# Linear attention beside a squared-ReLU layer: shorter warm-up, another start-up order, and two bursts moved ahead of the first gate pair

## The chip, the cores and the metric

One NeuronCore of a Trainium2 chip runs the whole program. The metric is the device time of one execution in microseconds. The times given are a median over several runs; the profile is one more execution, with every instruction recorded.

## What is computed

The input has 2048 tokens of 448 features. After a layernorm, one branch is linear attention with 16 heads of 28 features, the other a dense layer of 1792 units with a squared ReLU, whose output passes a SiLU and gates the first branch. The sum with the input is returned.

```python
xn = layernorm(x)                                  # no scale, no shift
q, k, v = split(xn @ wqkv)                         # 16 heads of 28
phi = lambda t: where(t > 0, t + 1, exp(t)) + 1e-6
kv, z = einsum("bhsd,bhse->bhde", phi(k), v), sum_s(phi(k))
s = ((phi(q) @ kv) / (phi(q) @ z + 1e-6)) @ wo     # heads joined before wo
h = relu(xn @ w1 + b1) ** 2
g = silu(h @ w2 + b2)
return x + s * g
```

## The kernel before

The 2048 tokens are 16 tiles of 128, and four groups (g = 0 to 3) of four tiles. For each tile the kernel needs the normalised tokens transposed, `xT`: 448 features are three chunks of 128 and a rest of 64, which is stored twice so that it can sit in either half of the partitions. `w1` is cut by output into 14 units `H0` to `H13` of 128, the queries into `Q0` to `Q2`, the keys into one unit `K` per tile.

**How work is written down.** The class `Program` holds operations with the tiles that they read and write. `place()` puts them on the engines. The order on TensorE (PE) and on the DMA queue of SyncE (SP) is the order of the calls in the source. On VectorE (DVE), ScalarE (ACT) and GpSimd (POOL) a planner picks the next operation by estimated times: by the time at which the result is due (`late`), or by a priority (`prio`) where one is given; `lead` moves a due time earlier, `after` adds a dependency, and `mode` of a DMA is the rate that the planner reckons with. Some operations may go to either DVE or ACT. The eight PSUM banks are given out by the planner too. `emit()` then writes the instructions with semaphore waits. So a changed estimate moves instructions, and no others change.

**The stages around the change, in order of time:**

- *Warm-up.* `warm(n)` issues n matmuls of 512 columns on constants (L976), nine at once and two behind the statistics of tile 0.
- *Tiles 0 to 3.* x arrives tile by tile (`load_x`), the first 768 columns of w1 by rows (`load_rows`), all from SP but the first rows and b1, which ACT issues. For each tile DVE takes the statistics (L409, L412), ACT makes `rstd` (a logarithm, L417, and an exponential, L421), DVE normalises (L427), PE transposes three chunks (L470), and DVE and ACT copy them out of PSUM into `xT` (L478). `h_tile(si)` then multiplies tile si with chunks c = 0, 1, 2 of w1 for the six units H0 to H5 at once (L996), six matmuls of 128 columns for each c; the next tile's transposes are called between c = 1 and c = 2. `h_rests` adds the 64-row rests (L1011).
- *Tiles 4 to 15.* `ln_group(g)` does statistics and normalisation on DVE, two tiles at a time, and transposes by DMA from SP (L455), one DMA for two tiles. The DMAs that are called before it stand ahead of it in SP's queue.
- *Bursts.* `fours("Q0 Q1|Q2 H3'", 0)` runs four units in both halves of PE's rows, in four parts of 8, 8, 6 and 6 matmuls (L610 for H, L552 for K, L576 for Q; the prime means the next group). It takes four PSUM banks. An H unit is followed by a relu on ACT (L592; for H0 to H5 of group 0 it may be on DVE, L589) and a square (DVE L598 or ACT L599); a K or Q unit by an exponential on ACT (L530) and two operations on DVE (L535, L540).
- *Gates.* `gates(a, c, inside)` computes h @ w2 for two tiles in two parts of 28 matmuls (L863), with a burst called between the parts. The first pair needs all of group 0's squared units and all 14 row blocks of w2. `g_out` (L844) adds b2 on DVE.

The order after the heads was:

```python
load_w2(0, 7, [pr.writer["xT3"]])
ln_group(1, lambda: load_w2(7, 14))   # the second half of w2 between the two transposes
load_x(8, 12)
late_loads()
fours("H6 H7|H10 H11", 0)
...
fours("Q0 Q1|Q2 H3'", 0)
g01 = gates(0, 1, lambda: fours("K4 H0|K5 H4", 1))
fours("H1 Q0|H5 Q1", 1)
```

Of the kernel before, what the change touches and what calls it, by code (L numbers as in the profile page):

```python
# [9 lines left out]
P = 128  # L10
S, D, F = 2048, 448, 1792
# [25 lines left out]
class Program:  # L37
# [9 lines left out]
    def add(self, eng, emit, reads=(), writes=(), dur=0.2, alts=(), nbytes=0, mode=None, after=(), prio=None, lead=0.0):  # L47
        op = Op(eng, emit, reads, writes, {eng: dur, **dict(alts)}, mode, nbytes, after)
        for t in op.reads:
            w = self.writer.get(t)  # L50
            if w is not None:
                op.deps.add(w)
            self.readers.setdefault(t, []).append(op)
        for t in op.writes:
            w = self.writer.get(t)
            if w is not None and w is not op:
                op.deps.add(w)
            for r in self.readers.get(t, ()):
                if r is not op:
                    op.deps.add(r)  # L60
            self.writer[t] = op
            self.readers[t] = [r for r in self.readers.get(t, ()) if r is op]
        op.deps.discard(op)
        for d in op.deps:
            d.succ.append(op)
        op.prio, op.lead = prio, lead
        self.ops.append(op)
        return op
# [174 lines left out]
def bass_recurrent_scan__linear_attn_block__dense_activation_squared_relu__prompt_kernel(  # L243
    nc, A_x, A_wqkv, A_wo, B_x, B_w1, B_b1, B_w2, B_b2, out
):
    with ExitStack() as es:
        sb = lambda name, shape, dtype: es.enter_context(nc.sbuf_tensor(name, shape, dtype))
        bf, f32 = dt.bfloat16, dt.float32
        pr = Program()
        add = pr.add  # L250
# [16 lines left out]
        b2b = sb("b2b", [P, D], bf)  # L267
# [74 lines left out]
        def dma(eng, dst, src, writes, nbytes, reads=(), after=(), prio=None, rate=None):  # L342
            return add(
                eng, lambda e, _: e.dma_start(dst, src), reads, writes, 0.45 if eng == "sp" else 0.5, nbytes=nbytes,  # L344
                after=after, prio=prio, mode=rate,
            )

        def load_x(lo, hi):
            dma("sp", x_tok[:, lo:hi, :], x_r[:, lo:hi, :], [("x", i) for i in range(lo, hi)], (hi - lo) * P * D * 2)

        def load_main(w, src, name, lo, hi):
            dma(
# [4 lines left out]
        def load_rest(eng, w, src, name, half, lo, hi, prio=None):  # L357
            dma(eng, w[HALF[half], 3, lo:hi], src[384:448, lo:hi], [(name, half)], 128 * (hi - lo), prio=prio)

        add("act", lambda e, _: e.preload_act_table_set("natural_log_exp_and_others"), [], ["actw"], 0.05, prio=-9)  # L360
        def load_rows(eng, c, prio=None):
            dma(eng, w_1[:, c, 0:768], B_w1[c * P : (c + 1) * P, 0:768], [("w1a", "m", c)], 768 * 256, prio=prio)

        dma("act", b1r[:, :], B_b1.rearrange("(f p) -> f p", p=P), ["b1r"], F * 2, prio=-8.5)
        load_x(0, 1)
        load_rows("act", 0, -8)
        load_x(1, 2)
        load_rows("sp", 1)
        load_x(2, 3)
        load_rows("sp", 2)  # L370
        load_x(3, 4)
        load_rest("sp", w_1, B_w1, "w1a", 0, 0, 384)
        load_rest("sp", w_1, B_w1, "w1a", 1, 384, 768)
        load_x(4, 8)
        load_main(w_1, B_w1, "w1b", 768, 1792)
        load_rest("sp", w_1, B_w1, "w1b", 0, 768, 1280)
        load_rest("sp", w_1, B_w1, "w1b", 1, 1280, 1792)
# [3 lines left out]
        load_main(w_qkv, A_wqkv, "wq", 0, D)  # L381
        load_rest("sp", w_qkv, A_wqkv, "wq", 0, 0, D)
        load_rest("sp", w_qkv, A_wqkv, "wq", 1, 0, D)
        dma("sp", b2b[:, :], bass.AP(tensor=B_b2.tensor, offset=B_b2.offset, ap=[[0, P], [1, D]]), ["b2b"], P * D * 2)

        def load_w2(lo, hi, after=()):
            dma(
# [18 lines left out]

        def ln_stats(si, prio=None, after=()):
            add(
                "dve", lambda e, _: e.bn_stats(st6[:, si, :], x_tok[:, si, :]), [("x", si)], [("st", si)], 0.53,  # L409
                prio=prio, after=after,  # L410
            )
            add("dve", lambda e, _: e.bn_aggr(mv[:, si, :], st6[:, si, :]), [("st", si)], [("mv", si)], 0.07, prio=prio and 0.5)  # L412

        def ln_rstd(lo, hi, prio=None):
            c = slice(lo, hi)
# [9 lines left out]
        def ln_norm(si, prio=None):  # L425
            def norm(e, dst, src):
                return e.tensor_scalar(  # L427
                    out=dst, in0=src, scalar1=mv[:, si, 0:1], scalar2=rstd[:, si : si + 1], op0=ALU.subtract, op1=ALU.mult
                )

            add(
                "dve", lambda e, _: norm(e, xn[:, si, 0:D], x_tok[:, si, :]), [("x", si), ("mv", si), ("rstd", si)],
                [("xn", si)], 0.3, prio=prio,
            )
# [5 lines left out]
                [("xn", i) for i in ts], [("xd", i) for i in ts], 0.07 + 0.02 * (hi - lo), prio=prio,  # L440
            )

        def ln_group(g, between=None):
            for a in (4 * g, 4 * g + 2):
                if a % 4 and between:
                    between()
                ln_stats(a, after=[pr.writer[("xT", 3, 0)]])
                ln_stats(a + 1)
                ln_rstd(a, a + 2)
                ln_norm(a)  # L450
                ln_norm(a + 1)
                ln_twin(a, a + 2)
                add(
                    "sp",
                    lambda e, _, a=a: e.dma_start_transpose(  # L455
                        xT[:, a : a + 2, :, :].rearrange("p s c t -> p (s c) t"),
                        xn[:, a : a + 2, :].rearrange("p s d -> p (s d)"),
                    ),
                    [(n, i) for n in ("xn", "xd") for i in (a, a + 1)], [("xT", a), ("xT", a + 1)], 1.25,
                    nbytes=2 * P * 1024, mode=180e3, lead=1.8 if a % 4 == 0 else 0.0,  # L460
                )

        def pe_transpose(pieces, names, dst, name, alts, prio):
# [19 lines left out]
        def tile_transpose(si):  # L483
            pe_transpose([(si, 0), (si, 1)], [("xn", si)], xT[:, si, 0:2, :], ("xT", si, 0), ("dve", "act"), 0)
            pe_transpose([(si, 2)], [("xn", si)], xT[:, si, 2:3, :], ("xT", si, 1), ("act",), 0)
# [86 lines left out]
        def qq(g, m):  # L572
# [8 lines left out]
            done = lambda: phi(b, pqT[:, m, g * 512 : (g + 1) * 512], ("pq", g, m), 512)  # L581
            return Unit(b, xt_names(4 * g, 4) + W("wq"), mm, done)

        def h_out(b, g, fi):
            slot = r2[g][:, fi, :]

            def relu(e, eng):
                if eng == "dve":
                    return e.tensor_scalar(  # L589
                        out=slot, in0=ps(b)[:, 0:512], scalar1=b1f[:, fi : fi + 1], scalar2=0.0, op0=ALU.add, op1=ALU.max  # L590
                    )
                return e.activation(out=slot, in_=ps(b)[:, 0:512], func=AF.Relu, bias=b1f[:, fi : fi + 1])  # L592

            add("act", relu, [b, "b1f"], [("r2", g, fi)], 0.57, alts=[("dve", 0.66)] if g == 0 and fi < 6 else ())

            def square(e, eng):
                if eng == "dve":
                    return e.tensor_tensor(out=slot, in0=slot, in1=slot, op=ALU.mult)  # L598
                return e.activation(out=slot, in_=slot, func=AF.Square)  # L599

            add("dve", square, [("r2", g, fi)], [("r2", g, fi)], 0.31, alts=[("act", 0.5)])
# [366 lines left out]

        one = nc.const_aps.tensor(1.0, (P, 512), bf)

        def warm(n, after=()):
            b = Buf("W")

            def f(e, _):
                for _i in range(n):
                    last = e.matmul(ps(b)[:, 0:512], one[:, 0:P], one, start=True, stop=True)  # L976
                return last

            add("pe", f, list(after), [b], n * 0.4, mode="128")

        for si in range(4):
            ln_stats(si, 1 + si)
            ln_rstd(si, si + 1, 0)
            ln_norm(si, 1.5 + si)
        ln_twin(0, 4, 6)

        heads = [Buf("H") for _ in range(6)]

        def h_tile(si, inside=None):
            for c in range(3):  # L990
                if c == 2 and inside:
                    inside()

                def f(e, _, c=c):
                    for fi, b in enumerate(heads):
                        last = e.matmul(  # L996
                            ps(b)[:, si * P : (si + 1) * P], w_1[:, c, fi * P : (fi + 1) * P], xT[:, si, c, :],
                            start=(si == 0 and c == 0), stop=False, skip_group_check=True,
                        )
                    return last  # L1000

                reads = [("xT", si, c // 2), ("w1a", "m", c)] + (heads if si or c else [])
                add("pe", f, reads, heads, 6 * 0.056, mode="128")
# [28 lines left out]
                prio=6,  # L1032
            )

        warm(9)
        warm(2, [("mv", 0)])
        tile_transpose(0)
        for si in range(3):
            h_tile(si, lambda: tile_transpose(si + 1))
        b1_rows()  # L1040
        pe_transpose([(si, 3) for si in range(4)], [("xd", si) for si in range(4)], xT[:, 0:4, 3, :], "xT3", ("act",), 0)
        h_tile(3)
        h_rests()
        load_w2(0, 7, [pr.writer["xT3"]])
        ln_group(1, lambda: load_w2(7, 14))
        load_x(8, 12)
        late_loads()
        fours("H6 H7|H10 H11", 0)
# [1 line left out]
        fours("H9 K1|H13 K3", 0)  # L1050
        ln_group(2)
        fours("Q0 Q1|Q2 H3'", 0)
        g01 = gates(0, 1, lambda: fours("K4 H0|K5 H4", 1))
        fours("H1 Q0|H5 Q1", 1)
        ln_group(3)
        g23 = gates(2, 3, lambda: fours("H2 K6|H10 K7", 1))
        fours("H6 H7|H11 H12", 1)
        fours("H8 H9|H13 Q2", 1)
        fours("H0 K8|H3 K9", 2)
        gates(4, 5, lambda: fours("H1 Q0|H4 Q1", 2))  # L1060
# [65 lines left out]
```

## Time and profile before

| | us |
|---|---|
| time, median of 3 runs (lowest to highest) | 146.19 (145.95 to 146.28) |
| time of the profiled execution | 145.45 |
| span of its instructions | 143.3 |
| PE busy | 138.1 (96%) |
| DVE busy | 92.2 (64%) |
| ACT busy | 77.7 (54%) |
| first warm-up matmul | 0.84 |
| tile 0's transposes on PE | 5.44 |
| first matmuls of `h_tile` | 6.40 |
| first burst | 12.53 |
| DMA transposes of tiles 4, 5 and of 6, 7 issued | 15.12 and 18.94 |
| first gate pair | 25.67 |
| last matmuls end | 140.5 |

The span is what the trace covers; some 2 us of the execution's own time lie around it. Instructions are named by their line in the kernel before. A time to landing of a DMA is counted from its issue. In the timeline, the bracket at a line's end gives the idle time of the engine ahead of it and what ended that.

### The profile page before, as it was taken

To read this page: it belongs to the slowest core of one execution; us is meant where nothing else is said; L and a number is where in the kernel's file an instruction comes from. 1 tells how busy PE (TensorE), PEld (TensorE's weight loads), DVE (VectorE), ACT (ScalarE), POOL (GpSimd) and SP (SyncE) were. 2 spreads that over 40 slices of the span, in tenths; PEclk is the share of its full clock that TensorE was granted. 3 is DMA by queue.
4 is the path that set the end of the run, shared out by engine and by line. 5 is a ranking of instruction groups with operands and counts; after the bars stand their busy time and mean duration, and the time that the engine had idled before them with its cause. 6 is when DMAs were issued, how large, how long until landed. Compare 5 with 4: busy or idle time off the path is not lost.

```text
span 143.3 us, 3271 instructions
## 1 busy us (share of the span) xinstructions
PE 138.1 (96%) x1339; PEld 70.0 (49%) x1339; DVE 92.2 (64%) x224; ACT 77.7 (54%) x151; POOL 26.9 (19%) x46
## 2 busy tenths in 40 slices
PE   7899996999999999999999999999999999999992
PEld 2486442544544444445446444445544555554562
DVE  1789977899967465365274779700158929367963
ACT  3438995855854676527427999473189430303020
POOL 7200016105005004102200551000000005041520
PEclk9999999999999999999999999999999999999999
DMA  4999999911542000000000000004993001204242
GB/s 88 272 364 271 263 310 298 340 29 44 78 100 47 0 5 0 0 5 0 0 0 5 0 2 5 0 32 106 181 183 51 2 5 32 96 5 128 63 133 61
DMA packets 17762, 12.90 MB, mean 90 GB/s; under 512 B 7524, under 2 KB 16980, under 8 KB 17748
## 3 DMA queue, kind: packets, MB, share of 16 engines
q1 hardware_dynamic: 16500, 11.56, 30.5%
q10 hardware_dynamic: 1248, 1.15, 4.3%
q8 instruction: 10, 0.16, 0.5%
q14 instruction: 4, 0.03, 0.1%
HBM read 9.16 MB, written 1.97 MB: 78 GB/s over the span
## 4 chain that ended last, share of the span: by engine, by line
PE 90%; DMA 5%; DVE 1%; SPq 1%; ACT 1%; issue 0%
PE pb L863 26%; PE pb L610 26%; PE pb L672 6%; PE pb L552 6%; PE pb L576 6%; PE pb L933 6%; PE pb L886 4%; PE pb L996 3%; DMA xT<-xn 3%; DMA x_tok<-in_A_x_dram 2%; PE pb L960 1%; PE pb L646 1%; PE pb L677 1%; SPq L344 1%; PE pb L803 1%; PE pb L723 1%
## 5 line engine op out<-in xcount | busy, mean ns | idle before, releaser
L610 PE MATMUL pb<-xT,w 64*128 64x512 bf16 x350 | 46.2, 376 | 0.0
L592 ACT ACTIVATE r<-pb,b1f 128x512 bf16<-128x512 f32 x53 | 34.3, 691 | 18.3 <-PE pb L610 17.7
L863 PE MATMUL pb<-w,r 64*128 64x448 bf16 x392 | 39.0, 349 | 0.0
L598 DVE TENSOR_TENSOR r<-r 128x512 bf16<-128x512 bf16 x40 | 17.8, 461 | 19.8 <-ACT r L592 19.8
L610 PEld LDWEIGHTS pb<-xT,w 64*128 64x128 bf16 x350 | 18.8, 94 | 19.3 <-DVE r L589 0.2
L863 PEld LDWEIGHTS pb<-w,r 64*128 64x128 bf16 x392 | 19.0, 94 | 18.5 <-PE pb L828 0.4
L564 POOL TENSOR_TENSOR zacc<-zacc,pk 128x448 f32<-128x448 f32 x13 | 13.6, 1050 | 49.3 <-DVE pk L540 48.8
L850 ACT ACTIVATE gbuf<-gbuf 128x448 bf16<-128x448 bf16 x15 | 8.0, 578 | 21.6 <-DVE gbuf L844 20.2
L922 POOL TENSOR_TENSOR gbuf<-gbuf,x_tok 128x448 bf16<-128x448 bf16 x7 | 7.2, 1034 | 44.1 <-DVE gbuf L918 44.0
L576 PE MATMUL pb<-xT,w_qkv 64*128 64x512 bf16 x84 | 14.4, 376 | 1.1 <-DMA xT<-xn 1.1
L918 DVE TENSOR_TENSOR gbuf<-pb,gbuf 128x448 bf16<-128x448 f32 (+2 forms) x17 | 9.2, 592 | 9.0 <-PE pb L933 7.4
L552 PE MATMUL pb<-w_qkv,xT 64*128 64x448 bf16 x112 | 14.5, 349 | 0.0
L409 DVE BATCH_NORM_STATS2 st<-x_tok 128x6 f32<-128x448 bf16 x16 | 9.8, 615 | 4.4 <-DMA x_tok<-in_A_x_dram 4.3
L599 ACT ACTIVATE r<-r 128x512 bf16<-128x512 bf16 x16 | 9.9, 629 | 0.3
L672 PE MATMUL pb<-pk,xn 128*128 128x448 bf16 x48 | 9.4, 353 | 0.0
L540 DVE SCALAR_TENSOR_TENSOR pk<-pb,pk 128x448 bf16<-128x448 f32 x16 | 9.3, 617 | 0.1
L844 DVE TENSOR_TENSOR gbuf<-pb,b2b 128x448 bf16<-128x448 f32 x15 | 8.6, 614 | 1.0 <-PE pb L863 0.6
L530 ACT ACTIVATE pk<-pb 128x448 bf16<-128x448 f32 x16 | 7.9, 541 | 2.2 <-PE pb L552 1.7
L552 PEld LDWEIGHTS pb<-w_qkv,xT 64*128 64x128 bf16 x112 | 6.1, 94 | 5.6
L576 PEld LDWEIGHTS pb<-xT,w_qkv 64*128 64x128 bf16 x84 | 5.3, 94 | 6.3 <-DMA xT<-xn 1.6
L540 DVE SCALAR_TENSOR_TENSOR pqT<-pb,pqT 128x512 bf16<-128x512 f32 x12 | 8.2, 687 | 0.3
L933 PE MATMUL pb<-msb,pqT 64*128 64x448 bf16 x72 | 8.3, 349 | 0.0
(81 smaller groups left out, 121.7 us busy)
## 6 DMA issues: line engine op xcount, KB each, us to landing
out_dram<-gbuf SPq DMA_DIRECT2D x15, 112.0 KB, 1.8
w<-in_B_w_dram SPq DMA_DIRECT2D x2, 784.0 KB, 5.9
x_tok<-in_A_x_dram SPq DMA_DIRECT2D x3, 448.0 KB, 4.4
w_qkv<-in_A_wqkv_dram SPq DMA_DIRECT2D x3, 336.0 KB, 6.1
w<-in_B_w_dram SPq DMA_DIRECT2D x1, 768.0 KB, 6.2
w_o<-in_A_wo_dram SPq DMA_DIRECT2D x1, 672.0 KB, 6.0
r<-rden_scratch SPq DMA_DIRECT2D x6, 112.0 KB
r<-rden_scratch ACTq DMA_DIRECT2D x5, 112.0 KB
```

Source lines behind the costliest of these rows:

```text
L409: "dve", lambda e, _: e.bn_stats(st6[:, si, :], x_tok[:, si, :]), [("x", si)], [("st", si)], 0.53,
L540: lambda e, _: e.scalar_tensor_tensor(out=slot, in0=ps(buf)[:, 0:n], scalar=1.0 + 1e-6, in1=slot, op0=ALU.add, op1=ALU.max),
L552: return e.matmul(ps(b)[:, 0:D], xT[rows, si, c, :], w_qkv[rows, c, D : 2 * D], start=start, stop=stop)
L564: return e.tensor_tensor(out=o[:, dst : dst + n], in0=first[:, src : src + n], in1=pk[:, si, src : src + n], op=ALU.add)
L576: return e.matmul(ps(b)[:, 0:512].rearrange("p (s t) -> p s t", s=4), w_qkv[rows, c, m * P : (m + 1) * P], xT[rows, 4 * g : 4 * g + 4, c, ...
L592: return e.activation(out=slot, in_=ps(b)[:, 0:512], func=AF.Relu, bias=b1f[:, fi : fi + 1])
L598: return e.tensor_tensor(out=slot, in0=slot, in1=slot, op=ALU.mult)
L599: return e.activation(out=slot, in_=slot, func=AF.Square)
L610: return e.matmul(ps(b)[:, 0:512].rearrange("p (s t) -> p s t", t=P), w_1[rows, c, fi * P : (fi + 1) * P], xT[rows, ts, c, :], start=start ...
L672: last = e.matmul(ps(b)[:, 0:D], xn[:, si, c * P : (c + 1) * P], pk[:, si, :], start=(si == 0), stop=(si == NT - 1),)
L863: last = e.matmul(ps(b)[:, 0:D], r2[si // 4][HALF[h], fi, t], w_2[HALF[h], fi, :], start=(part == 0 and fi == 0), stop=(part == 1 and fi = ...
L933: return e.matmul(ps(b)[:, 0:D], ap[c][rows, :], msb[rows, c, :], start=start, stop=stop)
```

## The change

- The warm-up is eight matmuls of 512 columns, four of 128 behind tile 0's statistics, and three of 128 behind its `rstd`. They were nine and two, all of 512.
- For tiles 0 to 3 the priorities of the aggregation and the normalisation, the estimate for the statistics and the rates of five early DMAs are other numbers. With them DVE's order becomes: statistics of tiles 0 and 1, norm 0, copy of tile 0, norm 1, statistics 2 and 3, norm 2, and so on; the copy of tile 1's first two chunks goes from DVE to ACT. Tile 1's transposes are called after c = 0 of tile 0.
- x of tiles 4 to 7 is issued ahead of the two rests of w1's first part.
- w2 comes in parts of 5 and 9 blocks, where it was 7 and 7, and both DMA transposes of tiles 4 to 7 stand between them; b2 is issued after w2, where it was ahead of it.
- In `ln_group` tile 7's statistics wait for the relu of H2 in group 0; the statistics of the second tile of the other pairs wait, as those of the first, for tile 3's copy. Lead times for group 1 are 4.0 and 4.0. On DVE three statistics of tiles 4 to 6 now come ahead of its first relu, and DVE has two of the six relus, where it had three.
- Two bursts, K4 H0|K5 H4 and H1 Q0|H5 Q1, are ahead of gate pair (0, 1). The first was inside it, the second after it. Inside it is now H6 H7|H11 H12, which came after gate pair (2, 3). So the second part of pair (0, 1) is followed at once by the first part of pair (2, 3).

```diff
+        load_rows("act", 0, -8, rate=170e3)
+        load_x(1, 2, rate=160e3)
+        load_rows("sp", 1, rate=560e3)
+        load_x(2, 3, rate=280e3)
         load_rows("sp", 2)
         load_x(3, 4)
+        load_x(4, 8)
         load_rest("sp", w_1, B_w1, "w1a", 0, 0, 384)
         load_rest("sp", w_1, B_w1, "w1a", 1, 384, 768)
-        load_x(4, 8)
...
-                [("x", si)], [("st", si)], 0.53,
+                [("x", si)], [("st", si)], 0.53 if prio is None else 0.63,
-            ... [("mv", si)], 0.07, prio=prio and 0.5)
+            ... [("mv", si)], 0.07, prio=prio and (0.0, 0.3, 0.3, -0.5, 2.7)[prio])
...
                 ln_stats(a, after=[pr.writer[("xT", 3, 0)]])
-                ln_stats(a + 1)
+                ln_stats(a + 1, after=[relus[0, 2]] if a == 6 else [pr.writer[("xT", 3, 0)]])
-                    nbytes=2 * P * 1024, mode=180e3, lead=1.8 if a % 4 == 0 else 0.0,
+                    nbytes=2 * P * 1024, mode=180e3, lead=lead[a % 4 // 2],
...
-        def warm(n, after=()):
+        def warm(n, after=(), cols=512):
-                    last = e.matmul(ps(b)[:, 0:512], one[:, 0:P], one, start=True, stop=True)
+                    last = e.matmul(ps(b)[:, 0:cols], one[:, 0:P], one[:, 0:cols], start=True, stop=True)
...
-            ln_norm(si, 1.5 + si)
+            ln_norm(si, 0.6 + si)
...
-        def h_tile(si, inside=None):
+        def h_tile(si, pos=None, inside=None):
             for c in range(3):
-                if c == 2 and inside:
+                if c == pos:
                     inside()
...
-        warm(9)
-        warm(2, [("mv", 0)])
+        warm(8)
+        warm(4, [("mv", 0)], P)
+        warm(3, [("rstd", 0)], P)
         tile_transpose(0)
-        for si in range(3):
-            h_tile(si, lambda: tile_transpose(si + 1))
+        for si, pos in enumerate((1, 2, 2)):
+            h_tile(si, pos, lambda: tile_transpose(si + 1))
...
-        load_w2(0, 7, [pr.writer["xT3"]])
-        ln_group(1, lambda: load_w2(7, 14))
+        load_w2(0, 5, [pr.writer["xT3"]])
+        ln_group(1, (4.0, 4.0))
+        load_w2(5, 14)
+        load_b2()
         load_x(8, 12)
         late_loads()
...
         fours("Q0 Q1|Q2 H3'", 0)
-        g01 = gates(0, 1, lambda: fours("K4 H0|K5 H4", 1))
+        fours("K4 H0|K5 H4", 1)
         fours("H1 Q0|H5 Q1", 1)
+        g01 = gates(0, 1, lambda: fours("H6 H7|H11 H12", 1))
         ln_group(3)
         g23 = gates(2, 3, lambda: fours("H2 K6|H10 K7", 1))
-        fours("H6 H7|H11 H12", 1)
         fours("H8 H9|H13 Q2", 1)
```

## The prediction

> **What bounds the kernel now.** I read the page first: TensorE (PE) is busy for 138.1 of 143.3 us, so every microsecond outside that is a place to look, and nothing else is.
>
> ```profile
> span 143.3 us, 3271 instructions
> PE 138.1 (96%) x1339; PEld 70.0 (49%) x1339; DVE 92.2 (64%) x224; ACT 77.7 (54%) x151; POOL 26.9 (19%) x46
> ```
>
> The 5.2 us that are left are 0.84 before the first matmul, 2.8 after the last one (140.5 to 143.3), and two waits, which the view of who waited for whom gives for PE:
>
> ```profile
> PE pb L576 <- DMA xT<-xn: 1.1, 1, 1.1
> PE pb L996 <- DVE xT L478: 0.6, 1, 0.6
> ```
>
> The chain that ended last names what stands behind each. Columns are start, length, what.
>
> ```profile
> 2.19 3.31 DMA x_tok<-in_A_x_dram
> 5.50 0.02 issue
> 5.53 0.63 DVE st L409
> 6.15 0.20 DVE xT L478
> ...
> 6.40 0.84 PE pb L996 x12
> ...
> 18.02 0.69 ACT r L592
> 18.71 0.23 ACT pk L530
> 18.94 4.35 DMA xT<-xn
> 23.29 0.05 issue
> 23.34 0.39 PE pb L576
> ```
>
> First place: VectorE (DVE) sits in tile 2's statistics, which wait for its x to land at 5.50, and only then copies tile 0's transposed columns, which PE had ready at 5.77. Second place: the second DMA transpose of tiles 4 to 7 is issued at 18.94 and lands at 23.29, while PE wants it for H3'. After 23.34 the chain is PE alone, gapless to 140.5. Whatever PE gains up to there should reach the end one for one.
>
> The timeline shows the warm-up:
>
> ```profile
> 0.84 4.76 PE L976 MATMUL pb<-const-bfloat16-1.0 128*128 128x512 bf16 x11 [0.84 <-PEq L1111]
> 4.50 0.36 DVE L427 TENSOR_SCALAR xn<-x_tok,mv,rstd 128x448 bf16<-128x448 bf16 x1
> 5.44 0.33 PE L470 MATMUL pb<-ident,xn 128*128 128x128 bf16 x3
> 6.07 0.27 DVE L478 COPY xT<-pb 128x256 bf16<-128x256 bf16 x1
> ```
>
> The eleven warm-up matmuls start 0.427 us apart, half the speed of later ones (a 512-column pair in a burst takes 0.216). The three transposes after 5.44 already run at full speed. Tile 0 was normalised at 4.86, so warm-up delayed its transposes by about 0.5 us.
>
> **The change, part by part.** Times below are of the profiled execution.
>
> *Warm-up.* Eight long matmuls end at 0.84 + 8 x 0.427 = 4.26. Seven of 128 columns cost a quarter, 7 x 0.107 = 0.75: end 5.01. Their waits (the statistics done at 3.85, rstd at 4.41) are over when PE arrives. If a 0.15 us weight load shows behind each, the end is 5.31; I take 5.01, as later 128-column matmuls hide theirs. Transposes then start at 5.0 instead of 5.44.
>
> *DVE order, tiles 0 to 3.* The copy of tile 0 now precedes tile 2's statistics. Transposes from 5.01 at the slow spacing have the second finished by 5.41, the copy (0.27) runs 5.45 to 5.72, and the first block of six matmuls starts at 5.78 instead of 6.40: 0.62 earlier. Part is given back. Tile 1's copy goes to ScalarE (ACT); 256 columns lie between its rows of 0.28 (128) and 0.60 (512), about 0.39, done at 6.81, before PE asks at 6.95. Then tile 2: norm of tile 1 to 6.0, statistics 6.54, aggregate 6.75; ACT is copying until 7.0, so Ln 0.29 and Exp 0.20 end at 7.48; the norm ends at 7.9 and PE, free since 7.62, waits until 7.95. It waited nowhere there before (8.42), so the lead is 0.47. From there the chain repeats: tile 2's copy by DVE at 8.54, tile 3's norm 9.13, its copy 9.85, b1's transpose at 9.9 (before 10.43), the 64-row finish (L1011) at about 11.34 against 11.87, the first burst (L610) at 12.0 against 12.53: 0.53.
>
> *Issues on SP up to there.* Tiles 4 to 7 of x (448 KB) now stand ahead of two 48 KB rests of w1. Everything to w1's last rest stays the same in bytes. That rest was issued at 6.49 and took 5.9 us (DMA view: 12.3 to 12.4), which today hides behind the L1011 matmuls and at 12.0 would not. Against that, the queue ran thin in before:
>
> ```profile
> 6.00:6.50 0.50, 0.10 (x2) 0.10 (x3) 0.50 (x4) 0.12 (x2) 0.00 (x0) 1.00 1.27 155
> 6.50:7.00 0.50, 0.50 (x11) 0.50 (x11) 0.50 (x2) 0.46 (x2) 0.00 (x0) 1.00 0.45 88
> ```
>
> The last column is GB/s; its neighbours have 279 and 326. The hole (about 0.5 us of transfer) falls where the small rests were served and the big x load was just starting. Issued 1.2 us earlier, that load should fill some of it. Bounds for the rest's landing: 12.3 (nothing filled) to 11.5; I take 11.9. Bounds of this stage's gain: 0.1 to 0.55; I take 0.45. The moved rests themselves are wanted at 11.3 and land by 9.3, where the x load did.
>
> *DVE after the heads.* Three statistics (0.56 each) now stand before DVE's first relu: from 10.28 to 12.0, relu done at 12.65. The burst's second half needs that PSUM bank at 12.0 + 0.86, so it just fits; were it late, a few tenths of PE.
>
> *Tiles 4 to 7.* Continue on DVE: relu, aggregates and a second relu to 13.6, tile 7's statistics 14.35, two squares 0.7, four norms 1.4 (a pair took 0.70), twins: 16.7. Both transposes are issued there, at 16.75 and 18.05 (1.3 us of SP each), the second 0.9 earlier than now. The two in before took 4.3 with a w2 half ahead of them in the queue; four later ones took 2.7, 3.4, 2.7, 2.7 without. In after only w2's first five blocks (560 of the former 784 KB) are ahead, with b2 gone from before them; the former part landed at 18.4, this one should by about 17.2. So I go by the 2.7 to 3.4 rows: landing 20.8 to 21.5. PE wants it where the second pair of Q units begins, 22.09 now, 21.6 after the lead. The wait, 23.34 - 22.09 = 1.25 us from start to start, is gone. By the 4.3 rows the landing would be 22.4, leaving 0.8.
>
> *Behind the transposes on SP* stand w2's other nine blocks, b2, x 8 to 15, wo and wv. They are issued from 19.4; 1008 KB at about 370 GB/s land by 24 to 25. The first gate pair moves from 25.67 to about 30 because two bursts of 3.0 now precede it, so w2 has 5 us to spare; without that move w2 would have been the new stall. x 8 to 11 lands about 2 us later, and its transposes follow, but their tiles are used near 51 and today land by 39.8.
>
> *The bursts moved ahead* are the same instructions: no PE time. H6 H7|H11 H12 moves inside the gate pair; two gate parts then lie back to back, with banks freed during the 2.65 us of each part. DVE is the risk: it was busy 9.88 of 10 us from 30 to 40. But its work is unchanged, a bank is wanted about a burst (3.0) after its matmuls ended, and the statistics of tiles 8 to 15 can slide. I cost it at zero; if that cover fails, one late PSUM read, 0.6 us.
>
> *Sum:* 0.45 + 1.25 = 1.7 us. Span 143.3 - 1.7 = 141.6, time 145.45 - 1.7 = 143.75 for that execution. It ran 0.74 below the median of the runs, 146.19, so the forecast is 146.19 - 1.7, 144.5 us.
>
> **A rule that speaks against it.** When PE turned fast is read from spacing: 0.43 until 5.06, 0.055 after 5.44, some 4.5 us after its first matmul. The Trainium skill, page "TensorE: Matmul & The Clock Gate", Part 4, says that transposes do not count as busy for the clock gate as matmuls do, and Part 1 that the gate looks at free-running windows of about 3.4 us. By these, ending the real matmuls at 5.0 could miss the window that closed near 5.4, and the next closes near 8.8; the 3.0 us from 5.78 would do 1.5 of work, and the sum would be 1.25 + 0.5 - 1.5, a gain of about 0.25 us. The trace shows only that transposes themselves ran fast, not what they count for.
>
> **The rivals.**
> 1. *A wait is only shortened* (27%). Either w1's rest lands at 12.3 (gain 0.1 there), or the second transpose takes 4.3 again (gain 0.45 of the 1.25). Gains: 0.1 + 1.25 = 1.35 down to 0.1 + 0.45 = 0.55: 144.8 to 145.6. For it: both durations stand in before. Against: the queue ahead is shorter in both cases.
> 2. *Slower: PE stays at half speed* (7%). Shorter warm-up plus the idle gap to 5.78 does not bring full speed, and another 4.5 us of activity is needed, to 10.3. The 4.5 us then do 2.25 of work: first burst 2.25 - 0.5 = 1.75 later, wait for tiles 4 to 7 gone (1.25): 0.5 slower, 146.7. It decides once the slow stretch passes 5.78 + 3.5 = 9.3. Against: the gap shrinks from 0.63 to about 0.4, and PE is busy without a break from 0.84 to about 5.3.
> 3. *No difference* (6%): PE arrives earlier at the same landings, and DVE, full between 24 and 40 with two bursts packed together, holds banks and takes back what remains: 145.9 to 146.5.
>
> **How the numbers follow.** The full gain has 60%; its own range is 1.4 to 1.9, 144.3 to 144.8. Faster, by over 0.2% (0.3 us, about what a measurement of this kernel can tell from no change): 60 + 27 = 87%. Same 5%, slower 8% (rival 2 and the tail of 3). The range runs from 144.1 (gain 1.9, and 0.2 for the spread of the runs) to 145.6, the end of rival 1.
>
> **What would show it.** Right: L996 starts near 5.8, L610 near 12.0, the transposes are issued near 16.8 and 18.1 and no DMA stands before PE near 21.6; the PE share rises above 96%. Wrong: L996 matmuls 0.107 apart past 6; PE waiting for w before L610; a wait between 24 and 46 with DVE or ACT behind it; a gate waiting for w2.

## The result, and the profile after

The changed kernel takes 144.44 us (median of 4 runs, 144.35 to 145.31); the kernel before takes 146.24 in the same comparison (145.95 to 146.45). The ratio is 0.9892, with a 95% interval from 0.985 to 0.9934. The forecast was 144.5. Here and below a ratio leaves out executions with a disturbed clock, so it can differ a little from the quotient of the medians beside it.

The number is right, but the profile shows only half of the way that was forecast. The page's first lines:

```profile
span 142.8 us, 3280 instructions
PE 137.8 (96%) x1343; PEld 70.4 (49%) x1343; DVE 90.8 (64%) x223; ACT 77.5 (54%) x152; POOL 27.2 (19%) x46
```

This execution took 144.53 us, that of before 145.45. Of the 0.92 between them only 0.5 lies in the span (142.8 against 143.3). What PE waited for, from the view of waits (total, times, longest):

```profile
PE pb L987 <- PEq L1125: 0.8, 1, 0.8
PE pb L621 <- DMA w<-in_B_w_dram: 0.8, 1, 0.8
PE pb L479 <- DVE xn L436: 0.4, 1, 0.4
PE pb L1007 <- DVE xT L487: 0.3, 1, 0.3
```

The wait of 1.1 us for tiles 4 to 7 is gone. The wait for tile 0's copy is half of what it was. But two new waits stand there, and the larger one is for w1 ahead of the first burst. (Lines are shifted: warm-up L976 is now L987, PE's transposes L470 are L479, `h_tile` L996 is L1007, the rests L1011 are L1022, bursts L610 and L576 are L621 and L585, DMA transposes L455 are L464, the gates L863 are L874; in e6, e7, e10 and e11 they stand one line further down.) The chain that ended last says the same (start, length, what):

```profile
6.51 6.71 DMA w<-in_B_w_dram
13.26 4.06 PE pb L621 x36
```

The timeline, for the steps of the prediction:

```profile
4.95 0.52 PE L479 MATMUL pb<-ident,xn 128*128 128x128 bf16 x3
...
5.41 0.29 DVE L487 COPY xT<-pb 128x256 bf16<-128x256 bf16 x1 [0.73 <-PE pb L479]
...
5.76 0.51 PE L1007 MATMUL pb<-xT,w 128*128 128x128 bf16 x6 [0.28 <-DVE xT L487]
...
7.18 0.63 DVE L418 BATCH_NORM_STATS2 st<-x_tok 128x6 f32<-128x448 bf16 x1 [0.43 <-DMA x_tok<-in_A_x_dram]
7.73 0.38 DVE L436 TENSOR_SCALAR xn<-x_tok,mv,rstd 128x448 bf16<-128x448 bf16 x1
...
8.16 0.34 PE L479 MATMUL pb<-ident,xn 128*128 128x128 bf16 x3 [0.39 <-DVE xn L436]
...
11.62 0.82 PE L1022 MATMUL pb<-xT,w 64*128 64x512 bf16 x6
...
13.26 4.06 PE L621 MATMUL pb<-xT,w 64*128 64x512 bf16 x36 [0.82 <-DMA w<-in_B_w_dram]
...
16.41 2.69 SPq L464 DMA_TRANSPOSE xT<-xn  x2
...
21.96 1.24 PE L585 MATMUL pb<-xT,w_qkv 64*128 64x512 bf16 x9
```

`h_tile` starts at 5.76 (forecast 5.78). Then the lead melts: tile 2's transposes at 8.16 where 7.95 was expected, the rests at 11.62 where 11.34 was, and the first burst at 13.26, where 12.0 was expected and before had 12.53. So the first burst is 0.73 later than in before, not 0.53 earlier. The transposes of tiles 4 to 7 are issued together at 16.4 and land at 19.27 and 20.60, and the Q burst at 21.96 runs through.

The two shifts make the whole difference: 1.25 won at the transposes, 0.73 lost at the first burst, 0.5 left, as the spans say. This sum holds in every profiled execution used below: the span, less the start of the first burst, less PE's extra waits behind it, is 129.5 to 129.6 us.

| profiled execution | first burst | waits of PE behind it | span | remainder |
|---|---|---|---|---|
| before | 12.53 | 1.25 | 143.3 | 129.5 |
| before again (e8) | 12.47 | 2.30 | 144.3 | 129.5 |
| after | 13.26 | 0 | 142.8 | 129.5 |
| after again (e9) | 13.46 | 0 | 143.0 | 129.5 |
| late half only (e1) | 12.58 | 0 | 142.1 | 129.5 |
| gate pair first again (e3) | 13.22 | 0.53 | 143.3 | 129.6 |
| w2 between the transposes again (e4) | 13.39 | 2.61 | 145.6 | 129.6 |
| x of 4 to 7 behind the rests again (e5) | 14.01 | 0 | 143.5 | 129.5 |
| x split (e6) | 12.60 | 0 | 142.1 | 129.5 |
| x split, old start-up (e7) | 12.66 | 0 | 142.2 | 129.5 |
| x split, four long warm-ups (e10) | 14.82 | 0 | 144.3 | 129.5 |
| x split, old warm-up (e11) | 12.74 | 0 | 142.3 | 129.5 |

A wait is counted as the spacing of two matmuls less the usual 0.22. As each timed run also has its span, a kernel without waits behind the first burst has its first burst at about the median span less 129.5; such figures are called estimates.

### The profile page after: what moved, and what is told of

It reads as the page before. It is cut to its first block, busy times and chain, and to the rows that moved or that the text cites. A ratio compares the mean times of both kernels' runs of the same rounds, so it can differ in the third digit from the quotient of the medians.

```text
span 142.8 us, 3280 instructions
## 1 busy us (share of the span) xinstructions
PE 137.8 (96%) x1343; PEld 70.4 (49%) x1343; DVE 90.8 (64%) x223; ACT 77.5 (54%) x152; POOL 27.2 (19%) x46
## 4 chain that ended last, share of the span: by engine, by line
PE 89%; DMA 5%; SPq 4%; issue 0%; DVE 0%; ACT 0%
PE pb L621 27%; PE pb L874 26%; PE pb L561 7%; PE pb L683 7%; PE pb L585 6%; PE pb L944 6%; DMA w<-in_B_w_dram 5%; PE pb L897 4%; SPq L344 4%; PE pb L971 1%; PE pb L657 1%; PE pb L688 1%; PE pb L814 1%; PE pb L734 1%; PE pb L839 1%
## 5 line engine op out<-in xcount | busy, mean ns | idle before, releaser
L621 PE MATMUL pb<-xT,w 64*128 64x512 bf16 x350 | 46.2, 376 | 0.8 <-DMA w<-in_B_w_dram 0.8
L603 ACT ACTIVATE r<-pb,b1f 128x512 bf16<-128x512 f32 x54 | 35.1, 691 | 20.7 <-PE pb L621 19.7
L874 PE MATMUL pb<-w,r 64*128 64x448 bf16 x392 | 38.9, 349 | 0.0
L621 PEld LDWEIGHTS pb<-xT,w 64*128 64x128 bf16 x350 | 18.8, 94 | 20.4 <-DMA w<-in_B_w_dram 1.3
L874 PEld LDWEIGHTS pb<-w,r 64*128 64x128 bf16 x392 | 19.0, 94 | 18.4 <-PE pb L839 0.4
L585 PE MATMUL pb<-xT,w_qkv 64*128 64x512 bf16 x84 | 14.2, 376 | 0.0
L610 ACT ACTIVATE r<-r 128x512 bf16<-128x512 bf16 x15 | 9.4, 635 | 0.3
L585 PEld LDWEIGHTS pb<-xT,w_qkv 64*128 64x128 bf16 x84 | 5.4, 94 | 4.9
```

Source lines behind the costliest of these rows:

```text
L585: return e.matmul(ps(b)[:, 0:512].rearrange("p (s t) -> p s t", s=4), w_qkv[rows, c, m * P : (m + 1) * P], xT[rows, 4 * g : 4 * g + 4, c, ...
L621: return e.matmul(ps(b)[:, 0:512].rearrange("p (s t) -> p s t", t=P), w_1[rows, c, fi * P : (fi + 1) * P], xT[rows, ts, c, :], start=start ...
L874: last = e.matmul(ps(b)[:, 0:D], r2[si // 4][HALF[h], fi, t], w_2[HALF[h], fi, :], start=(part == 0 and fi == 0), stop=(part == 1 and fi = ...
```

## The experiments

My theory after the result: the late half (w2, transposes, bursts) gives all of the gain, and the start-up half gives nothing or costs, because x of tiles 4 to 7 holds back w1's last rest. The rival: both halves give what was forecast, and the late first burst is an accident of one trace. Two more questions came with the runs: what the warm-up's length is worth, and how well one trace of before stands for its runs.

### Each half alone

**e1**: the start-up as before, the rest as after. Of the edit the main lines; the rates, priorities and estimates of tiles 0 to 3 are those of before too:

```diff
-        warm(8)
-        warm(4, [("mv", 0)], P)
-        warm(3, [("rstd", 0)], P)
+        warm(9)
+        warm(2, [("mv", 0)])
...
-        load_x(4, 8)
         load_rest("sp", w_1, B_w1, "w1a", 0, 0, 384)
         load_rest("sp", w_1, B_w1, "w1a", 1, 384, 768)
+        load_x(4, 8)
...
```

> Start-up as before; only the later half of the change: w2 in parts of 5 and 9 with both DMA transposes between, b2 late, two bursts ahead of the gate pair. Theory A (the wait for tiles 4 to 7 is all that this half removes, and the start-up half brings some 0.45 more): 1.25 us under before, no DMA wait of PE near 22, the rest of w1 landing at 12.3 to 13 behind the L1011 matmuls, first burst near 12.5. Theory B (the start-up half costs time, because x of tiles 4 to 7 goes ahead of w1): this kernel is as fast as the changed one or faster, 1.7 us or more under before.

Measured: 144.16 us (6 runs, 143.62 to 144.28), ratio 0.988 [0.9855, 0.9905]. PE's waits are only these:

```profile
PE pb L987 <- PEq L1124: 0.8, 1, 0.8
PE pb L1007 <- DVE xT L487: 0.3, 1, 0.3
```

w1's last rest landed at 12.54, and the first burst ran at 12.58. That is theory B: the late half alone gives at least all that the whole change gives.

**e2**: the other half. `load_w2`, `ln_group` and the order of bursts and gate pair as before, the start-up as after.

```diff
-        load_w2(0, 5, [pr.writer["xT3"]])
-        ln_group(1, (4.0, 4.0))
-        load_w2(5, 14)
-        load_b2()
+        load_w2(0, 7, [pr.writer["xT3"]])
+        ln_group(1, lambda: load_w2(7, 14))
...
```

> Only the start-up half: warm-up, VectorE order of tiles 0 to 3, rates, x of tiles 4 to 7 ahead of the two rests; w2, transposes and bursts as before. Theory A: first matmuls of h_tile near 5.8, first burst at 12.0 unless w1's last rest lands later; the wait for tiles 4 to 7 is still there and takes back what was gained, since the second transpose still lands where it did, so 0 to 0.4 us under before. Theory B: w1's last rest lands after 12.8, first burst later than before, 0.3 us or more over before.

Measured: 146.05 (12 runs), ratio 0.9998 [0.9975, 1.0021]. The start-up half is worth nothing by itself, the lower end of theory A's 0 to 0.4. That does not yet mean that it costs nothing in the whole change: here the wait for tiles 4 to 7 still stands behind it, and by the sum above a first burst that starts later only shortens that wait (argued: the timed runs have only spans, median 144.0 against 143.9). e1 against after shows the price: its first burst at 12.58 against 13.26.

### The late half in parts

**e3**: after, with the first gate pair ahead of the two bursts again.

```diff
-        fours("K4 H0|K5 H4", 1)
+        g01 = gates(0, 1, lambda: fours("K4 H0|K5 H4", 1))
         fours("H1 Q0|H5 Q1", 1)
-        g01 = gates(0, 1, lambda: fours("H6 H7|H11 H12", 1))
...
+        fours("H6 H7|H11 H12", 1)
```

> The changed kernel with only the order of bursts and gates put back (first gate pair directly behind Q0 Q1|Q2 H3'). Theory A: the second part of w2 lands near 25.5 while PE arrives at the gate near 24.4 to 25.8, so PE waits for w2 by 0 to 1.2 us: 0 to 1.2 us over the changed kernel, DMA of w2 named as releaser. Rival: w2 is in time, the two bursts ahead of the gates are worth nothing, same time as the changed kernel within 0.2 us.

Measured: 145.23 (12 runs, 144.9 to 145.75), ratio 0.9944 [0.9917, 0.9972]: 0.8 over after (0.7 over the ten runs of after that there are with e9). The waits name it, w2 ahead of the first gate:

```profile
PE pb L874 <- DMA w<-in_B_w_dram: 0.4, 1, 0.4
```

w2's nine blocks landed at 25.44; PE's spacing there was 0.75 (24.73 to 25.48), 0.53 more than usual. So the moved bursts, costed at nothing, hide this stall, as the prediction said of them.

**e4**: after, with w2 in halves and the second between the two transposes.

```diff
-        load_w2(0, 5, [pr.writer["xT3"]])
-        ln_group(1, (4.0, 4.0))
-        load_w2(5, 14)
+        load_w2(0, 7, [pr.writer["xT3"]])
+        ln_group(1, (4.0, 4.0), lambda: load_w2(7, 14))
```

> The changed kernel with w2 again in parts of 7 and 7 and the second half between the two transposes. Theory A: the second transpose is issued behind 784 KB of w2 and lands 4.3 us after its issue, near 22.3 to 23.3; the wait of PE for tiles 6 and 7 returns with 0.5 to 1.5 us, so 0.5 to 1.5 us over the changed kernel. Rival (the earlier normalisation alone removes the wait, and the queue does not matter): same time as the changed kernel within 0.3 us.

Measured: 147.9 (6 runs, 147.54 to 149.32), ratio 1.0171 [1.0113, 1.0229]: some 3 us over after (3.5 by these medians, 2.8 by the spans of the two profiled executions), twice the upper end of the 0.5 to 1.5 that was expected, and slower than before. From its timeline and its waits:

```profile
17.64 1.12 SPq L344 DMA_DIRECT2D w<-in_B_w_dram  x1
...
18.80 1.28 SPq L464 DMA_TRANSPOSE xT<-xn  x1
...
24.78 0.39 PE L585 MATMUL pb<-xT,w_qkv 64*128 64x512 bf16 x1 [1.66 <-DMA xT<-xn]
```

```profile
PE pb L585 <- DMA xT<-xn: 1.7, 1, 1.7
PE pb L621 <- DMA w<-in_B_w_dram: 1.1, 1, 1.1
...
PE pb L585 <- DVE pqT L549: 0.5, 1, 0.5
```

The second transpose is issued at 18.80, 1.2 behind 784 KB of w2 in the same queue. It lands at 24.73, 5.9 us later (4.3 was expected), where after's was issued at 17.81 and took 2.8. This costs 1.8 at Q, and two smaller waits follow near 30 (0.15 and 0.65, one of them for DVE). With the first burst 0.13 later this is 2.7 of the 2.8 us between the spans. The order of transposes and w2 is the part that carries the change.

### Where one trace of before stands

**e8**: before once more, one look.

> The kernel before once more, for a second trace: its first one was of a run (145.45) below most others (median 146.2). Theory: the wait for tiles 4 to 7 near 22 varies with the landing of the transpose behind w2's second half and is 1.3 to 2.2 us from start to start, first burst at 12.5 to 12.8. Rival: the first burst is what varies, with w1's last rest landing near 13.

Measured: 146.41 us, span 144.3. The same wait is twice as long as in the first trace:

```profile
PE pb L576 <- DMA xT<-xn: 2.1, 1, 2.1
```

```profile
18.89 5.40 DMA xT<-xn
```

The second transpose was issued at 18.89 as in the first trace (18.94) and took 5.4 us, not 4.35, with w2's second half landing at 22.48, not 21.54. The spans of 38 undisturbed runs of before in the three comparisons lie from 143.4 to 145.6, median 143.9. The trace that the prediction was made from, 143.3, is below them all. By the sum above a wait of about 1.9 us is usual (143.9 - 129.5 - 12.5, an estimate).

### The order of x and w1's rests

**e5**: after, with x of tiles 4 to 7 behind the two rests, as in before. All else of the start-up is new.

```diff
-        load_x(4, 8)
         load_rest("sp", w_1, B_w1, "w1a", 0, 0, 384)
         load_rest("sp", w_1, B_w1, "w1a", 1, 384, 768)
+        load_x(4, 8)
```

> The changed kernel with only x of tiles 4 to 7 put back behind the two 48 KB rests of w1's first part; VectorE order and warm-up stay new. Theory B (x ahead of the rests is what delays the rest of w1's second part, which landed at 13.0 to 13.3 in four traces with x ahead, and at 12.3 and 12.5 in two with x behind): that rest lands at 12.3 to 12.6, first burst at 12.4 to 12.7 instead of 13.3, 0.5 to 0.8 us under the changed kernel, about 143.8. Rival (the landing differs from run to run, not by the order): it lands at 12.3 to 13.3 as it comes, within 0.3 us of the changed kernel.

Measured: 143.92 (7 runs, 143.49 to 145.57), ratio 0.9841 [0.9799, 0.9884]. w1's last rest landed at 12.14. The profiled execution is the slowest of the seven, for another reason, told below. The median span is 141.9, so the first burst is usually near 12.4 (estimate), as theory B has it.

**e9**: after once more, against the suspicion that its trace was an accident.

> The changed kernel once more, on the same chip as the next two. Theory B (x ahead of the rests holds w1's last rest to 13.0 to 13.4 and with it the first burst): the L1022 matmuls start at 11.4 to 11.7, the first burst at 13.1 to 13.4; 144.2 to 144.6. Rival: the profiled run of the changed kernel was an exception, the first burst starts by 12.6 and most runs are near 143.8.

Measured: 144.68 (6 runs, 144.13 to 145.59), ratio 0.9891 [0.9838, 0.9943]. The rest landed at 13.41 and the first burst ran at 13.46. It was no accident. The rests of `h_rests` began at 12.25, later than the 11.4 to 11.7 expected: x of tile 3 landed at 7.79, and tile 2's transposes ran at 8.79. Without the wait for w1 the first burst of this execution would have come near 12.9 (12.25 and the usual 0.66, an estimate), so w1 is not the whole of its delay. (The view of waits names a relu on DVE here, which ended at 13.43; the semaphore that PE waited for last, reached at 13.41, is that of the load.) w1's last rest landed at 13.18 to 13.41 where x of tiles 4 to 7 stood ahead of the small rests (after, e3, e4, e9), and at 12.14 to 12.54 where it stood behind them (before, e8, e1, e5).

How this comes about shows in part in the windows of the DMA engines (from after, then from e5; the last two columns are the share of time that the DMA engines were busy and GB/s):

```profile
6.00:7.00 1.00, 1.00 (x22) 1.00 (x20) 0.72 (x3) 0.58 (x3) 0.00 (x0) 1.00 0.99 350
7.00:9.00 2.00, 1.61 (x26) 1.27 (x24) 1.36 (x5) 1.01 (x5) 0.00 (x0) 1.00 0.91 263
9.00:11.00 2.00, 2.00 (x35) 1.81 (x33) 1.47 (x5) 0.56 (x2) 0.00 (x0) 1.00 0.89 270
```

```profile
6.00:7.00 1.00, 0.72 (x8) 0.63 (x8) 0.97 (x3) 0.28 (x1) 0.00 (x0) 1.00 1.01 166
7.00:9.00 2.00, 2.00 (x21) 2.00 (x20) 1.34 (x5) 0.97 (x5) 0.00 (x0) 1.00 0.96 365
9.00:11.00 2.00, 2.00 (x28) 1.83 (x26) 0.62 (x2) 0.63 (x3) 0.00 (x0) 1.00 1.07 348
```

The hole at 6 to 7 us is filled, as hoped: 350 GB/s against 166. But the four microseconds after it run at 263 and 270 against 365 and 348, and this returns more than was won. All four traces with x ahead show it (243 to 292 between 7 and 11), the four others do not (348 to 366). The bytes asked for are the same. Why the rate falls stays open. The share of time in which the DMA engines were busy falls too (0.91 and 0.89 against 0.96 and 1.07), but by less than the rate, and no run here says why.

**e6**: the order that these readings suggest: x of 4 and 5 behind the small rests, x of 6 and 7 behind w1's second part, and tile 6's statistics as late as tile 7's.

```diff
-        load_x(4, 8)
         load_rest("sp", w_1, B_w1, "w1a", 0, 0, 384)
         load_rest("sp", w_1, B_w1, "w1a", 1, 384, 768)
+        load_x(4, 6)
         load_main(w_1, B_w1, "w1b", 768, 1792)
         load_rest("sp", w_1, B_w1, "w1b", 0, 768, 1280)
         load_rest("sp", w_1, B_w1, "w1b", 1, 1280, 1792)
+        load_x(6, 8)
...
-                ln_stats(a, after=[pr.writer[("xT", 3, 0)]])
+                ln_stats(a, after=[relus[0, 2]] if a == 6 else [pr.writer[("xT", 3, 0)]])
```

> As the run before (new warm-up and VectorE order, rests first), and x of tiles 6 and 7 goes behind w1's second part, their statistics behind the relu of H2. If the start-up gain is only hidden by w1's landing, then with 224 KB less ahead w1's last rest lands at 11.6 to 12.0, the first burst starts at 12.1 to 12.2, and the time is 0.3 to 0.5 us under the run with x only put back, about 143.4. If w1's landing does not decide, same as that run. Danger: tiles 6 and 7 are normalised later, the second DMA transpose is issued at 18 and must land by 21.9.

Measured: 143.66 (6 runs, 143.06 to 144.64), ratio 0.983 [0.9786, 0.9875]. The last rest landed at 11.76, as expected, and the first burst started at 12.60 straight after the rests of `h_rests`, without a wait for w1. It was expected at 12.1 to 12.2, and by the median span of 141.7 it usually is near 12.2 (estimate); in this execution x of tile 1 landed late (4.49), and tile 0's transposes ran only at 5.70. The DMA transposes were issued at 16.55 and 17.95, about as in after. This is the best of the kernels run, 0.8 below after.

**e7**: the same order of x, with warm-up, priorities and rates of before.

```diff
-        warm(8)
-        warm(4, [("mv", 0)], P)
-        warm(3, [("rstd", 0)], P)
+        warm(9)
+        warm(2, [("mv", 0)])
...
```

> Warm-up and VectorE order of tiles 0 to 3 as before, the later half new, x of tiles 6 and 7 behind w1's second part. With w1 out of the way the old start-up sets the first burst, near 12.5 as in the kernel before: 0.3 to 0.5 us over the run with the new start-up and the same x order, equal to the run with the later half alone within 0.2 (144.1). If the two are equal, the new warm-up and VectorE order bring nothing even where w1 does not hold them.

Measured: 144.01 (6 runs, 143.92 to 144.31), ratio 0.9852 [0.9816, 0.9888]; rest landed 11.44, first burst 12.66. It overlaps with e6, so the rest of the start-up half (shorter warm-up, new order on DVE) is worth about 0.3, near what these runs can tell.

### The warm-up

In e5's profiled execution PE was at half speed for long. `h_tile`'s 24 matmuls there, and in e6:

```profile
7.31 2.76 PE L1007 MATMUL pb<-xT,w 128*128 128x128 bf16 x24
```

```profile
6.88 1.50 PE L1008 MATMUL pb<-xT,w 128*128 128x128 bf16 x24
```

The matmuls of e5 are 0.107 apart until 9.93, where those of e6 are 0.06 apart or less from about 4.3. In e5 x of tile 1 had landed late (4.39 against 3.50 in after), and two gaps in PE's work followed, matmuls 0.75 and 0.60 apart (4.85 to 5.60, 5.78 to 6.38). On DVE the statistics of tile 1 stand ahead of tile 0's normalisation, in before as in after, so a late x of tile 1 holds up tile 0's transposes: they ran at 5.60 here, 5.70 in e6 and 5.71 in e10, later than the 5.44 of before. Then the earlier end of the warm-up wins nothing. The long half speed is rival 2 of the prediction: first burst at 14.01. The six other runs of e5 have spans up to 142.2, so it is not the rule. The next two runs change the warm-up of e6 only.

**e10**: four long matmuls instead of eight.

```diff
-        warm(8)
+        warm(4)
```

> The kernel with x split (143.66) with four long warm-up matmuls instead of eight; the seven short ones stay. PE then idles from 2.55 to about 3.8. Theory C (PE gets its full clock at the end of a stretch of about 3.4 us in which it was busy most of the time, and the stretches run freely against the start): full speed comes in many runs one stretch later, at 6.6 to 10, matmuls 0.107 apart until then, first burst 0.5 to 1.7 later, runs spread by over 1 us, median 144.2 to 145.2. Rival: the warm-up is long enough in either case, full speed by 6.6 and the same time within 0.3.

Measured: 145.1 (12 runs, 144.05 to 146.3), ratio 0.9909 [0.9875, 0.9943]: 1.4 over e6, and 1.1 over e11, which was run beside it. Its profiled execution, the slowest of the twelve:

```profile
0.84 1.86 PE L988 MATMUL pb<-const-bfloat16-1.0 128*128 128x512 bf16 x4 [0.84 <-PEq L1126]
3.89 1.06 PE L988 MATMUL pb<-const-bfloat16-1.0 128*128 128x128 bf16 x7 [1.18 <-DVE mv L422]
...
7.42 2.77 PE L1008 MATMUL pb<-xT,w 128*128 128x128 bf16 x24
```

PE idles for 1.18 us between the two parts of the warm-up; full speed comes at 11.86, and the first burst at 14.82, both beyond what was expected (6.6 to 10, and at most 1.7 over e6's 12.60). By the median span of 143.2 the first burst is usually near 13.7 (estimate); that the other executions lose it in the same way is argued, as this trace is the only one. So a shorter warm-up can cost more than all that its early end brings.

**e11**: nine and two long ones, as in before.

```diff
-        warm(8)
-        warm(4, [("mv", 0)], P)
-        warm(3, [("rstd", 0)], P)
+        warm(9)
+        warm(2, [("mv", 0)])
```

> The kernel with x split (143.66) with the warm-up of before, nine and two long matmuls; VectorE order stays new. Theory: transposes of tile 0 start at 5.48 in every run, 0 to 0.5 later than with the short matmuls, so 0 to 0.4 us over 143.66, and the runs lie closer together (within 0.5) since full speed always comes by 6.6. Rival: the short matmuls bring the whole 0.35 between the run with x split and the same with the old start-up (144.01), so this one is at 144.0.

Measured: 143.97 (6 runs, 143.4 to 144.42), ratio 0.9837 [0.9792, 0.9882]; first burst 12.74. It is like e7 (144.01), so DVE's new order alone is worth nothing that can be measured, and the new warm-up about 0.3, within the spread of the runs. The runs with the new warm-up also spread more: spans from 141.3 to 142.9 in e6 and 141.6 to 143.5 in e5, against 141.9 to 142.3 in e1 and 142.0 to 142.5 in e7 with the old one. But e11, which has the old one too, lies from 141.6 to 142.5; its times, expected within 0.5, lie 1.0 apart, and its full speed came at 6.8, not by 6.6. So the spread is not shown to be the warm-up's alone.

## Why the prediction was right, and where it was not

The time, 144.44 against 144.5, is right partly by luck: two terms of the sum were off in opposite directions. One of the prediction's own signs of being wrong, PE waiting for w ahead of the first burst, came (0.82 us).

- **Warm-up and DVE's order: right as far as they go.** Transposes at 4.95 (5.0 forecast), the copy at 5.41 (5.45), `h_tile` at 5.76 (5.78). What this is worth where w1 does not hold the first burst is some 0.3 (e6 against e7), and by e11 it is the warm-up's.
- **Tile 2: wait too small.** 7.95 was forecast, 8.16 measured, and 8.00 to 8.79 in the four traces of this start-up (after, e3, e4, e9). The prediction left x of tile 3 where it was (6.42). With x of tiles 4 to 7 directly behind it, it landed at 6.78 to 7.79, and its statistics stand ahead of tile 2's norm on DVE.
- **w1's last rest: this step failed.** It gave bounds of 11.5 to 12.3 for the landing and took 11.9, as the earlier x load "should fill some of the hole". The hole was filled, but the rate fell behind it, and the rest landed at 13.21. The start-up term, +0.45, became -0.73 in this trace. By median spans, e5 against after shows what the order of x costs, by w1's rest and by x of tile 3 together: 141.9 against 142.8 (ten runs), 0.9. The other start-up edits bring 0.25 (e5 against e1, 142.15) to 0.5 (e6 against e7, 141.7 and 142.2). So the forecast of 0.45 would have fitted the start-up without this one move, as far as these runs can tell.
- **The transposes: mechanism right, size too small.** They were forecast at 16.75 and 18.05 and to land by 20.8 to 21.5; they were issued at 16.42 and 17.81 and landed at 19.27 and 20.60, so the 2.7 to 3.4 rows were the right ones, and by e4 w2 ahead of a transpose is what had made it slow. But 1.25 was the wait of one quick execution of before: 2.30 in e8, about 1.9 as a rule. The prediction noted that this execution was 0.74 below the median, and took the same gain off the median all the same; part of what lay between them was this wait.
- **The sum.** By median spans: about 1.9 for the transposes, less 0.65 for the start-up (13.3 - 12.65, after and e1), less about 0.15 for e1's first burst against before's, is 1.1, which is 143.9 - 142.8. This is bookkeeping, no test: the 1.9 comes from the same spans. The predicted 1.25 + 0.45 = 1.7 came out close for other reasons. The times differ by 1.8 in the first comparison and 1.4 over all undisturbed runs (145.97 against 144.57); what lies around the span varies by a few tenths too (1.73 and 2.15 us in the two profiled executions).
- **w2 and the bursts: right.** w2's nine blocks were issued at 19.15 (19.4) and landed at 25.59 (24 to 25 forecast), and the gates began at 31.0 (about 30 forecast). e3 shows the stall that the move avoids. x of tiles 8 to 11 landed at 28.74 (24.37 in before, so 4.4 later, not 2), which nobody felt. No wait stood between 24 and 46, so rival 3's mechanism did not occur.
- **Rival 1**, in its first half, is what happened to w1's rest, beyond the bound that it had there. Rival 2 occurred now and then, as said: full speed at 9.93 in e5 (10.3 in the rival), first burst 1.4 later than in e6 (1.75).
- **The rule on the clock.** Full speed came between about 3.6 us (e8) and 6.8 us (e11) in the traces where it came early: 4.3 in e6, 5.4 in before, between 5.2 and 5.8 in after, about 6.0 in e1, 6.3 in e3, 6.6 in e7. So the rule did not cost the 1.5 us in after. Then it came twice about one such spread later, at 9.93 and 11.86, where PE had idled for over 1.1 us before. The Trainium skill, "TensorE: Matmul & The Clock Gate", Part 1, tells of free-running windows of about 3.4 us and of a transition that varies by half a microsecond either way from run to run; the spread here, 3.2 us, agrees with the window and not with that half. Whether transposes count for the gate (Part 4 of that page) was not isolated: in both late cases there was idle time as well.

## What to carry to other kernels

A DMA that PE will wait for goes ahead of the bulk loads in its queue, and the consumer of the bulk is moved later by as much as the bulk loses: this pair carries the gain here (some 3 us are lost without the first, e4, and 0.7 to 0.8 without the second, e3). When a start-up is shortened, look for the landing that sets the next stage, and do not put a large load ahead of it on the ground that the queue has a hole. A wait read from one execution is one draw; where its execution is off the median, look at that wait first.

## What was not expected of the hardware

- The second DMA transpose of tiles 4 to 7 took 2.8 us with no load issued in the 6 us ahead of it in the queue (after, e3, e9, e5, e6, e7, e10, e11; 3.6 in e1), and 4.35, 5.4 and 5.9 us behind 784 KB that were issued 1.2 to 2.4 us ahead of it in the same queue (before, e8, e4). A clear queue is no guarantee: in after two later transposes, issued at 35.79 and 37.08 after more than 2 us without DMA traffic, took 4.10 and 3.65.
- Moving one 448 KB load ahead of two of 48 KB, with all bytes the same, put off the landing of another load by 0.6 to 1.3 us, and for 4 us the DMA rate was 243 to 292 GB/s, where it was 348 to 366.
- The moment when PE reaches full speed differs by 3.2 us between executions of nearly the same first 5 us, and it came 3 to 5 us later still where PE had been idle for a microsecond.
